# Four tokens to a partition for q and k, and seven block products for eight in the token mix, in a chunked attention and wave-MLP kernel

## The chip, the core and the metric

The kernel runs on one core of a Trainium2 chip. A core has TensorE (matrix products, PE in the profile, with its weight loads as PEld), VectorE (DVE), ScalarE (ACT), GpSimd (POOL) and SyncE (SP), a working memory of 128 partitions, and accumulator memory (PSUM) of eight banks, each of 512 f32 values per partition. Transfers run on 16 DMA engines; here GpSimd issues the loads that change f32 to f16, SP and ScalarE issue the rest. The metric is the time of one execution on the device in microseconds, lower is better; kernels are compared by medians of several executions.

## The reference

q, k and v have the shape 8 x 8 x 576 x 64 (batch, head, token, depth). Attention is done within chunks of 64 tokens; the result is laid out as batch x 576 x 512 and goes through a token and channel mixing block.

```python
scores = scale * np.matmul(q_c, k_c.transpose(0, 1, 2, 4, 3))   # chunks of 64 tokens
attn = np.exp(scores - max); attn = attn / (sum + 1e-9)
x = np.matmul(attn, v_c)                                        # then (8, 576, 512)
theta = x @ w_theta
zr, zi = x * np.cos(theta), x * np.sin(theta)
y = einsum('ts,bsd->btd', w_tok_r, zr) + einsum('ts,bsd->btd', w_tok_i, zi)
u = x + y
out = u + np.maximum(u @ w_ch, 0.0)
```

## The kernel before

The eight batches are worked in four pairs, 0 to 3. The 2 x 576 tokens of a pair are five groups: A and B are the first and the second 256 tokens of the pair's first batch, C and D those of its second batch, each two tiles of 128 tokens; M is the middle tile, the last 64 tokens of both batches.

Nothing is scheduled by a planner at run time. The text `ORDER` (line 16) lists every step, and the loop at line 769 issues them in that order; each engine runs its own instructions in the order of the list and waits for the others by semaphores. A step reads `name.pair+group.banks`, so `L.0C.1.2` is the step L for group C of pair 0 with PSUM banks 1 and 2. A digit after the name is a part: for most steps half of the heads (0 or 1) or one of the two tiles.

A group goes through these steps, in the names of the list:

- `q`, `k` (load_qk, line 172) and `v` (load_v, line 204): loads on GpSimd's queue, eight of them in flight at a time. q and k come with two adjacent tokens on a partition, 128 partitions, so that a packet holds two tokens of a head (256 B as f16); v comes one token to a partition in three loads per group. From the second pair on each load first copies a recent reciprocal (`gate`, line 166), which holds the queue back until that attention is done. q and k of a group share a buffer from a pool of ten, which also serves raw weights, outputs of the last pairs and, where they are used, differences of z.
- `L` or `T` or `N` (qk_t, line 284): transposes of q and k on TensorE. L is the long form, 32 transposes of a 128x64 piece; T is the small form, 64 transposes of 64x64, four of which fit side by side on the array; N is for M. `tq`, `tkA`, `tkV` (qk_copy, line 327) bring the results out of PSUM on VectorE or ScalarE.
- `S` (scores, line 345), `e` (exps, on ScalarE), `V` (attn: products with v and a column of ones), `n` (norm, on VectorE: a reciprocal and a multiplication, giving x).
- `X`, `Q` (turn: x transposed, in the long and the small form), `xA`, `xV` (its copy), `H` (x times w_theta), `g` (cosine and sine on ScalarE), `z` (two products on VectorE).
- `Y` (line 542; `YA` to `YM` by source group): the token mix. A group's output takes 18 matmuls of 128x128 by 512 columns (two tiles, each four tiles of tokens for the real and four for the imaginary part, and one for M); `Y.pM` takes 18 on half the array. `y` (add_x, line 680) adds x from PSUM, giving u, on VectorE.
- `U`, `R` (turn u, long and small), `uA`, `uV`, `W` (u times w_ch), `w` (relu_add, line 685), `s`, `sA` (stores issued by SP and by ScalarE).

`lw`, `TW`, `twV`, `twA` load, transpose and copy the token weights; `lt`, `ct` and `lc` handle w_theta and w_ch; `pe` and `pg` load ScalarE's tables for exponentials and for sines ahead of time; `D.n` issues n matmuls of zeros, which compute nothing. The steps `jw`, `j`, `K` and `r` (lines 592 to 674) exist in the code but are not in the list before. Functions touched by the change are shown here.

## Time and profile before

| | us |
|---|---|
| median of three runs | 206.74 (206.2 to 206.82) |
| the profiled execution | 205.98 |
| its span, first to last instruction | 204.2 |
| TensorE, VectorE, ScalarE, GpSimd busy | 192.3, 126.0, 115.6, 89.3 |
| granted TensorE clock, mean | 0.995 |

The span is cut into 40 slices of 5.1 us on the page; a digit there is the busy share of an engine in tenths. In lists of groups, "128x1024 f16<-128x1024 f32 x14 | 17.0, 1224" means 14 instructions that write 128 partitions of 1024 f16 values from f32 values, busy for 17.0 us in all, 1224 ns each; what follows is the engine's idle time before them and what ended it. "issue" stands for time in which an engine waited for nothing that the profile shows. Busy time of TensorE is modelled from pipelined instructions; the distance from one step's first matmul to the next one's is the better price of a step. The packed trace also records each DMA packet and the landing of each load.

### The profile page before, as it was taken

How to read it: one execution, taken by the hardware profiler on the slowest of the kernel's cores; microseconds unless marked ns; L12 is line 12 of the kernel's file. 1: busy time of each engine (PE TensorE's matmuls, PEld its weight loads, DVE VectorE, ACT ScalarE, POOL GpSimd, SP SyncE). 2: the span in 40 equal slices, each digit the busy share in tenths (PEclk: the TensorE clock that was granted, in tenths of full speed). 3: DMA queues.
4: the chain of work that ended last, by engine and by line, in shares of the span. 5: the costliest groups of instructions: out<-in, count | busy, mean ns of one | idle time of the engine just before them, and what ended most of it. 6: DMA issues, size and time to landing. Idle time of an engine off the chain costs nothing.

```text
span 204.2 us, 7908 instructions
## 1 busy us (share of the span) xinstructions
PE 192.3 (94%) x3584; PEld 102.8 (50%) x3584; DVE 126.0 (62%) x226; ACT 115.6 (57%) x142; POOL 89.3 (44%) x130
## 2 busy tenths in 40 slices
PE   7977999999997799999999999999999999999991
PEld 2344556656464365544654645445555544454440
DVE  0335696667364587924467886589666768643662
ACT  2044996678985378960759836498960857030120
POOL 7889495649989289999403502230400000000000
PEclk9999999999999999999999999999999999999997
DMA  6999999999999989999904993940723002042546
GB/s 210 144 150 150 179 190 169 146 181 118 169 170 157 114 158 176 167 173 159 122 11 127 214 256 135 157 27 3 51 59 106 3 3 104 0 167 108 190 177 185
DMA packets 87009, 27.00 MB, mean 132 GB/s; under 512 B 80064, under 2 KB 81984, under 8 KB 86976
## 3 DMA queue, kind: packets, MB, share of 16 engines
q0 software_dynamic: 81264, 16.01, 93.2%
q1 hardware_dynamic: 3920, 7.08, 10.2%
q10 hardware_dynamic: 1792, 3.41, 4.6%
q8 instruction: 28, 0.46, 0.9%
q14 instruction: 5, 0.04, 0.0%
HBM read 33.06 MB, written 9.44 MB: 208 GB/s over the span
## 4 chain that ended last, share of the span: by engine, by line
PE 76%; DMA 13%; POOL 5%; issue 4%; DVE 0%; DVEq 0%; POOLq 0%
PE ps L564 29%; PE ps L478 27%; DMA v<-in_v_dram 7%; DMA qk<-in_k_dram 4%; PE ps L550 4%; PE ps L438 3%; PE ps L318 3%; PE ps L400 3%; PE ps L447 3%; POOL qk L197 3%; PE ps L366 2%; DMA out_dram<-o 1%; POOL v L221 1%; POOL wnat L232 1%; PE ps L301 1%
## 5 line engine op out<-in xcount | busy, mean ns | idle before, releaser
L564 PE MATMUL ps<-z,wT 128*128 128x512 f16 x288 | 65.6, 380 | 1.5 <-issue 1.5
L564 PEld LDWEIGHTS <-wT 128*128 128x128 f16 x288 | 26.9, 98 | 32.6 <-issue 1.8
L221 POOL DMA_DIRECT2D v<-in_v_dram x48 | 36.2, 766 | 7.0 <-DMA qk<-in_k_dram 3.3
L683 DVE TENSOR_TENSOR x<-ps,x 128x1024 f16<-128x1024 f32 (+1 forms) x22 | 22.5, 1028 | 25.2 <-PE ps L564 22.4
L478 PE MATMUL ps<-wtheta,xT 128*128 128x512 f16 x144 | 34.4, 380 | 0.1
L478 PE MATMUL ps<-wch,uT 128*128 128x512 f16 (+1 forms) x148 | 34.1, 374 | 0.0
L382 ACT ACTIVATE eT<-ps 128x1024 f16<-128x1024 f32 (+1 forms) x18 | 16.6, 928 | 25.8 <-PE ps L366 24.4
L693 DVE SCALAR_TENSOR_TENSOR o<-ps,x 128x1024 f32<-128x1024 f32 (+2 forms) x23 | 22.5, 990 | 10.7 <-PE ps L478 6.6
L461 ACT COPY uT<-ps 128x1024 f16<-128x1024 f16 (+1 forms) x16 | 14.4, 909 | 25.5 <-PE ps L447 12.5
L414 DVE TENSOR_TENSOR x<-ps,recip 128x512 f16<-128x512 f32 (+1 forms) x40 | 25.5, 638 | 1.4
L338 ACT COPY kT<-ps 128x1024 f16<-128x1024 f16 (+1 forms) x18 | 16.4, 927 | 15.9 <-PE ps L305 10.8
L492 ACT ACTIVATE cos<-ps,pihalf 128x1024 f16<-128x1024 f32 (+1 forms) x22 | 21.2, 965 | 6.1 <-PE ps L478 3.5
L169 POOL COPY seen<-recip 1x1 f32<-1x1 f32 x13 | 2.7, 210 | 45.9 <-DVE recip L412 45.9
L478 PEld LDWEIGHTS <-uT 128*128 128x128 f16 x148 | 13.7, 98 | 15.0 <-issue 0.4
L478 PEld LDWEIGHTS <-xT 128*128 128x128 f16 x144 | 12.9, 98 | 13.8 <-issue 0.2
L496 ACT ACTIVATE sin<-ps 128x1024 f16<-128x1024 f32 (+1 forms) x22 | 19.2, 873 | 0.0
L334 DVE COPY qT<-ps 128x1024 f16<-128x1024 f16 (+2 forms) x23 | 12.9, 569 | 6.4 <-PE ps L305 4.4
L197 POOL DMA_DIRECT2D qk<-in_q_dram x16 | 14.5, 905 | 2.3 <-issue 1.5
L412 DVE RECIPROCAL recip<-ps 128x8 f32<-128x8 f32 (+1 forms) x40 | 7.9, 197 | 12.2 <-PE ps L400 10.3
L197 POOL DMA_DIRECT2D qk<-in_k_dram x16 | 14.4, 900 | 1.0 <-issue 0.6
L137 ACT ACT_TABLE_LOAD x11 | 14.1, 1283 | 0.2
L461 ACT COPY xT<-ps 128x1024 f16<-128x1024 f16 (+1 forms) x13 | 11.8, 922 | 1.3 <-PE ps L447 1.0
(52 smaller groups left out, 204.5 us busy)
## 6 DMA issues: line engine op xcount, KB each, us to landing
qk<-in_q_dram POOLq DMA_DIRECT2D x16, 256.0 KB, 6.4
qk<-in_k_dram POOLq DMA_DIRECT2D x16, 256.0 KB, 6.5
out_dram<-o SPq DMA_DIRECT2D x8, 512.0 KB, 3.6
out_dram<-o ACTq DMA_DIRECT2D x6, 512.0 KB, 3.3
v<-in_v_dram POOLq DMA_DIRECT2D x40, 64.0 KB, 5.5
v<-in_v_dram POOLq DMA_DIRECT2D x16, 128.0 KB, 6.2
wraw<-in_moe_w_theta_dram SPq DMA_DIRECT2D x2, 512.0 KB, 3.8
out_dram<-o SPq DMA_DIRECT2D x8, 128.0 KB, 2.3
```

Of the source, the lines that this page charges most:

```text
L197: nc.gpsimd.dma_start(t.rearrange("p (h x) -> p h x", h=H)[:, hs], ap[2 * p + bb, :, s0 : s0 + GT, :].rearrange("h (p s) d -> p h (s d)", ...
L221: nc.gpsimd.dma_start(v16[rows, slot + tile, :, 0:D], v[2 * p + bb, :, t0 : t0 + m, :].rearrange("h s d -> s h d"),)
L338: nc.scalar.copy(out=t.rearrange("p x s c -> p x (s c)").rearrange("p x (c s) -> p x c s", s=2), in_=ps.rearrange("p x s c -> p x c s"),)
L382: nc.scalar.activation(out=eT.rearrange("p h r e c -> p (h r e) c"), in_=ps, func=AF.Exp, scale=scale)
L414: nc.vector.tensor_tensor(out=tokens(p, g, "x")[:, :, f * NE * D : (f + 1) * NE * D].rearrange("p c (h d) -> p c h d", h=NE), in0=psv[:, 0 ...
L461: (nc.vector.tensor_copy if how == "V" else nc.scalar.copy)(out=to.rearrange("p b (r c) -> p b r c", c=CH), in_=psv)
L478: nc.tensor.matmul(ps[:, a * DM : a * DM + cols.stop - cols.start], xT[:, b0 + a, db, :], weight[:, db, cols], start=(db == 0), stop=(db = ...
L492: nc.scalar.activation(out=cos[:, 0:n].rearrange("p a e -> p (a e)"), in_=pin, func=AF.Sin, bias=pihalf, scale=1.0,)
L496: nc.scalar.activation(out=sin[:, 0:n].rearrange("p a e -> p (a e)"), in_=pin, func=AF.Sin)
L564: nc.tensor.matmul(ps[:, a * DM : a * DM + DM], wT[:, kt, t0 : t0 + P], zs[bb], start=(done + k == 0), stop=(done + k == NK - 1),)
L683: nc.vector.tensor_tensor(out=u, in0=ps, in1=u, op=ALU.add)
L693: nc.vector.scalar_tensor_tensor(out=o, in0=ps[:, 0 : n * m].rearrange("p (j d) -> p j d", j=n), scalar=0.0, in1=u, op0=ALU.max, op1=ALU.add,)
```

## The change

There are three parts.

**Loads of q and k.** For groups A to D the new steps `qF` and `kF` put four adjacent tokens on a partition. q takes partitions 0 to 63 of the buffer and k partitions 64 to 127. A load has 512 packets of 512 B instead of 1024 packets of 256 B, with the same bytes. M is loaded as before.

**Transposes.** Step `F` is a small form for this layout, 64 transposes of 64x64; `FL` is a long form, 32 transposes of a 128x64 piece that holds q above k. Scores read q with a stride of four tokens, and the copies and exponentials restore the order. `tqA` copies q on ScalarE.

**Token mix.** In pair 0 it stays as it is, by source group. In pairs 1 to 3 the two batches are mixed together, as a 2x2 matrix of 256-token blocks of the weights times the 2x2 blocks of z (A, C above B, D), by seven block products, as Strassen's method does, in Winograd's form. `jw` forms four sums of weight blocks once; `ja` to `jd` form four differences of z per pair on VectorE; `Ka` to `Kg` are the products of eight matmuls each, b, c and d of which add M's column in two more, and `Km` adds it for the fourth block; products add up in the same PSUM banks, and the takes `ra` to `rh` add them to x on VectorE in between. M itself is mixed by `Y` as before. These functions are unchanged and now used (cut to their core):

```python
ZSUMS = {"a": ("C", "A"), "b": ("D", "a"), "c": ("D", "C"), "d": ("B", "b")}   # first - second
PRODUCTS = {  # PSUM block, weight block or sum, z block or difference, M's column for (block row, batch)
    "a": ("x", (0, 0), "A", None),  "b": ("y", (0, 1), "B", (0, 0)),
    "c": ("z", 3, "D", (0, 1)),     "d": ("w", (1, 1), "d", (1, 0)),
    "e": ("z", 0, "a", None),       "f": ("x", 1, "b", None),
    "g": ("x", 2, "c", None),       "m": ("x", None, None, (1, 1)),
}
TAKES = {  # group whose x is added to, PSUM block
    "a": ("A", "x"), "b": ("A", "y"), "c": ("C", "x"), "d": ("C", "z"),
    "e": ("D", "z"), "f": ("D", "x"), "g": ("B", "x"), "h": ("B", "w"),
}
def weight_sums(i):   # jw.00, jw.01; put is one VectorE tensor_tensor into wsum[k], 128x1024
    if i == 0: put(0, w_block(1, 0), w_block(1, 1), ALU.add); put(2, w_block(0, 0), w_block(1, 0), ALU.subtract)
    else:      put(1, wsum[0], w_block(0, 0), ALU.subtract);  put(3, w_block(0, 1), wsum[1], ALU.subtract)
def step(p, g, bank):  # product k
    ...
    for a in range(2):
        ...
        for i, (wt, zt) in enumerate(terms):   # 4 terms of a product, and one of M's column
            nc.tensor.matmul(ps[:, a * DM : a * DM + DM], wt, zt,
                             start=fresh and i == 0, stop=i == len(terms) - 1, ...)
def step(p, g):        # take k
    nc.vector.tensor_tensor(out=u, in0=st[p]["ps_k", frm], in1=u, op=ALU.add)
```

**The order.** The whole list is another one. It loads and transposes B, C and D of the first pair ahead of M and A, has 36 dummy matmuls for 42, and ends with whole groups where the list before ended with halves. The diff, with the list cut:

```diff
--- before.py
+++ after.py
@@ -14,45 +14,47 @@
 ORDER = """
-q.0B k.0B init.00 D.12.0 lt.00 ctV1.00 ctV0.00 q.0M k.0M id.00 D.19.0 L0.0B.0.1 tkA0.0B
-L1.0B.7.6 tq1.0B N0.0M.5 tkV0.0M tkA1.0B q.0A N1.0M.1 tq0.0B S1.0B.6 tkV1.0M tq0.0M D.3.2
-S0.0M.2 e1.0B tq1.0M S0.0B.4 v.0B D.4.0 V1.0B.0 e0.0B e0.0M V0.0B.2 n0.0B k.0A S1.0M.6 D.4.5
-L1.0A.5.4 v.0M n1.0B L0.0A.3.2 tq1.0A e1.0M Q0.0B.0 tq0.0A tkA1.0A S1.0A.6 Q1.0B.4 tkA0.0A
...
-W1.3C.0 y.3M R.3M.4 uV1.3D s.3B R0.3D.2 w.3A y0.3C R0.3C.6 sA.3A W1.3D.1 w1.3C uV.3M w1.3D
-W.3M.0 uA0.3C s1.3C uA0.3D W0.3D.7 s1.3D w.3M s.3M w0.3D W3.3C.1 s0.3D w3.3C s3.3C W2.3C.0 w2.3C
-s2.3C
+init.00 D.12.0 qF.0B kF.0B id.00 D.14.0 F1.0B.0.1 qF.0C kF.0C F0.0B.2.3 tq1.0B tkA1.0B S1.0B.0
+FL.0C.4 tq.0C qF.0D kF.0D D.5.6 FL.0D.6 v.0B e1.0B tq0.0B tkA.0C S.0C.4 e.0C lt.00 tq.0D ctV0.00
+ctV1.00 v.0C D.5.4 V1.0C.4 tkA0.0B q.0M k.0M V0.0C.0 tkA.0D S.0D.2 n0.0C e.0D S0.0B.6 v.0D n1.0C
+N0.0M.0 tq0.0M qF.0A X.0C.1 N1.0M.2 e0.0B xV.0C V0.0B.6 tkA0.0M tqA1.0M V1.0B.4 n1.0B H.0C.0
+kF.0A n0.0B lw.00 v.0M V1.0D.4 v.0A FL1.0A.6 n1.0D lw.02 tkA1.0M pg.00 g.0C FL0.0A.2 V0.0D.4
+tq1.0A qF.1C tq0.0A tkA0.0A kF.1C n0.0D X0.0B.0 tkA1.0A S1.0M.2 X.0D.1 xV0.0B xV.0D TW.00.4
+twV.00 q.1M e1.0M TW.01.6 twV.01 S1.0A.0 z.0C qF.1A S0.0A.2 e0.0A V1.0M.4 n1.0M e1.0A H0.0B.5
+S0.0M.6 V0.0A.2 e0.0M n0.0A H.0D.0 V1.0A.6 V0.0M.4 pg.00 g.0D n1.0A kF.1A g0.0B YC.0C.2 n0.0M
+X.0M.4 xV.0M X0.0A.0 xV0.0A qF.1B TW.02.6 kF.1B H.0M.1 twV.02 Q1.0B.4 xA1.0B FL.1C.6 H1.0B.0
...
+qF.3A kF.3A sA.1B q.3M V0.3C.6 V0.2B.4 Y.1M.1 z.2A uA.1A V1.3C.2 n0.2B n0.3C Q.2B.4 xA.2B y.1M
+n1.3C Ka.2A.6 Q.2M.0 Q.3C.2 ja.2C s.0M s.1C xV.3C F.3A.5.4 xA.2M H.2M.0 tqA.3A k.3M ra.2A g.2M
+Ke.2C.2 W.1A.0 z.2D jb.2D re.2D w.1A tkA.3A S.3A.4 pe.00 e.3A z.2M jc.2D Kf.2C.6 H.2B.4 H.3C.0
+pg.00 g.2B Kc.2D.2 rc.2C F.3D.4.5 g.3C tkA.3D V1.3A.0 Kg.2D.6 U.1M.5 z.2B rd.2C v.3M n1.3A rg.2B
+tqA.3D V0.3A.0 n0.3A R.1D.2 uA.1D Y.2M.4 uV.1M V1.3B.0 n1.3B T.3M.2 tqA.3M y.2M X.3A.5 xA.3A
+Km.2D.6 tkV.3M W.1D.0 s.1A v.3D S.3D.2 V0.3B.4 rf.2D H.3A.6 pe.00 e.3D n0.3B w.1D R.2C.4 Q.3B.2
...
+pg.00 g.2B Kc.2D.2 rc.2C F.3D.4.5 g.3C tkA.3D V1.3A.0 Kg.2D.6 U.1M.5 z.2B rd.2C v.3M n1.3A rg.2B
+tqA.3D V0.3A.0 n0.3A R.1D.2 uA.1D Y.2M.4 uV.1M V1.3B.0 n1.3B T.3M.2 tqA.3M y.2M X.3A.5 xA.3A
+Km.2D.6 tkV.3M W.1D.0 s.1A v.3D S.3D.2 V0.3B.4 rf.2D H.3A.6 pe.00 e.3D n0.3B w.1D R.2C.4 Q.3B.2
+jd.2B xV.3B z.3C Kb.2B.0 rb.2A uA.2C g.3A W.1M.2 w.1M H.3B.4 g.3B V1.3D.0 n1.3D V0.3D.6 Kd.2B.2
+n0.3D Q.3D.0 z.3A S.3M.4 pe.00 e.3M W.2C.6 rh.2B V0.3M.2 n0.3M ja.3C V1.3M.5 xA.3D R.2B.3 uA.2B
+H.3D.0 pg.00 g.3D W.2B.2 n1.3M w.2C X.3M.4 xA.3M Ka.3A.6 w.2B z.3D jb.3D R.2D.0 R.2A.2 uA.2A
+uA.2D z.3B sA.2C s.2B Ke.3C.4 ra.3A re.3D H.3M.3 g.3M z.3M W.2A.0 W.2D.2 w.2D jd.3B w.2A Kf.3C.6
+rc.3C s.1D s.2D Kc.3D.4 Kd.3B.2 Kb.3B.0 jc.3D Kg.3D.6 rh.3B rb.3A R.3A.0 rd.3C uA.3A rg.3B
+Y.3M.2 sA.1M R.3B.0 uA.3B R.3C.4 Km.3D.6 y.3M rf.3D W.3A.2 W.3B.0 w.3A uA.3C sA.2A w.3B R.3D.6
+uA.3D s.3A R.2M.2 uA.2M W.3C.4 W.3D.6 w.3C w.3D R.3M.0 sA.3B W.2M.2 w.2M s.3C s.3D uA.3M W.3M.0
+w.3M sA.2M s.3M
 """.split()
@@ -174,6 +176,16 @@
         gate(p)
         if (p, g) not in nats:
             nats[p, g] = nat.tile([P, 2, 2 * DM], FP16, name="qk16", tag="nat")
+        if plain is None:
+
+            t = nats[p, g][half[which]].rearrange("p a x -> p (a x)")
+            nc.gpsimd.dma_start(
+                t.rearrange("p (h x) -> p h x", h=H),
+                (q, k)[which][2 * p + bb, :, s0 : s0 + GT, :].rearrange(
+                    "h (p s) d -> p h (s d)", s=4
+                ),
+            )
+            return
         t = nats[p, g][:, which]
         hs = slice(0, H) if f is None else slice(f * NE, f * NE + NE)
         ap = (q, k)[which][:, hs]
@@ -285,7 +297,38 @@
         n = 1 if g == "M" else 2
         ne, e0 = part(f)
         t = nats[p, g]
-        if form != "small":
+        if form == "four":
+
+            t = t.rearrange("p a x -> p (a x)")
+            pss = [psum(b, 1, FP16)[:, 0 : ne * 4 * CH] for b in banks]
+            pss = [ps.rearrange("p (e s c) -> p e s c", e=ne, s=4) for ps in pss]
+            for e in range(ne):
+                for s in range(4):
+                    for w in range(2):
+                        for h in range(2):
+                            x0 = ((2 * (e0 + e) + h) * 4 + s) * D
+                            nc.tensor.transpose(
+                                pss[w][half[h], e, s],
+                                t[half[w], x0 : x0 + D],
+                                id16[half[w], half[w]],
+                            )
+        elif form == "four long":
+
+            form = "four"
+            t = t.rearrange("p a x -> p (a x)")
+            ps = psum(banks[0], 2, FP16)[:, 0 : ne * 4 * P]
+            ps = ps.rearrange("p (e s w c) -> p e s w c", e=ne, s=4, w=2)
+            for e in range(ne):
+                for s in range(4):
+                    for h in range(2):
+                        x0 = ((2 * (e0 + e) + h) * 4 + s) * D
+                        nc.tensor.transpose(
+                            ps[half[h], e, s].rearrange("p w c -> p (w c)"),
+                            t[:, x0 : x0 + D],
+                            id16,
+                        )
+            pss = [ps[:, :, :, w] for w in range(2)]
+        elif form != "small":
 
             if n == 2:
                 pss = [psum(b, 1, FP16)[:, 0 : ne * n * P] for b in banks]
@@ -328,16 +371,16 @@
         ps = st[p]["ps_qkT", g, f][which]
         _, nx, n, c = ps.shape
         name = "qk"[which] + "T"
-        t = tmp.tile([P, nx, n, c], FP16, name=name, tag=f"{name}{n}")
+        t = tmp.tile([P, nx, n, c], FP16, name=name, tag=f"{name}{min(n, 2)}")
         st[p][name, g, f] = t
         if how == "V":
             nc.vector.tensor_copy(out=t, in_=ps)
-        elif n == 1 or st[p]["form", g, f] == "plain":
+        elif which == 0 or n == 1 or st[p]["form", g, f] == "plain":
             nc.scalar.copy(out=t, in_=ps)
         else:
             nc.scalar.copy(
                 out=t.rearrange("p x s c -> p x (s c)").rearrange(
-                    "p x (c s) -> p x c s", s=2
+                    "p x (c s) -> p x c s", s=n
                 ),
                 in_=ps.rearrange("p x s c -> p x c s"),
             )
@@ -357,8 +400,13 @@
                         x, r0 = (r * ne + e, 0) if form == "small" else (e, r)
                         k0 = (n * r0 + cc) * CH
                         i0 = r0 * CH + cc * CH // 2
-                        kc = kf[half[h], x, k0 : k0 + CH]
-                        if n == 1 or form == "plain":
+                        if form != "four":
+                            kc = kf[half[h], x, k0 : k0 + CH]
+                        if form == "four":
+                            k0 = (2 * r + cc) * CH
+                            kc = kf[half[h], e, k0 : k0 + CH]
+                            qc = qT[half[h], e, :, k0 // 4 : k0 // 4 + CH // 4]
+                        elif n == 1 or form == "plain":
                             qc = qf[half[h], x, k0 : k0 + CH]
                         else:
                             qc = qT[half[h], x, :, i0 : i0 + CH // n]
@@ -378,7 +426,8 @@
             )
             return
         if st[p]["form", g, f] != "plain":
-            ps = ps.rearrange("p x (s i) -> p x i s", s=2)
+            s = 4 if st[p]["form", g, f] == "four" else 2
+            ps = ps.rearrange("p x (s i) -> p x i s", s=s)
         nc.scalar.activation(
             out=eT.rearrange("p h r e c -> p (h r e) c"), in_=ps, func=AF.Exp, scale=scale
         )
@@ -736,10 +785,15 @@
         "kP": lambda p, g, f: load_qk(p, g, 1, True, f),
         "ctA": lambda p, g, f: cast_theta(f, nc.scalar.copy),
         "ctV": lambda p, g, f: cast_theta(f, nc.vector.tensor_copy),
+        "qF": lambda p, g, f: load_qk(p, g, 0, None, f),
+        "kF": lambda p, g, f: load_qk(p, g, 1, None, f),
+        "F": lambda p, g, f, *banks: qk_t(p, g, f, "four", *banks),
+        "FL": lambda p, g, f, *banks: qk_t(p, g, f, "four long", *banks),
         "T": lambda p, g, f, *banks: qk_t(p, g, f, "small", *banks),
         "L": lambda p, g, f, *banks: qk_t(p, g, f, "long", *banks),
         "N": lambda p, g, f, *banks: qk_t(p, g, f, "plain", *banks),
         "tq": lambda p, g, f: qk_copy(p, g, f, 0, "V"),
+        "tqA": lambda p, g, f: qk_copy(p, g, f, 0, "A"),
         "tkV": lambda p, g, f: qk_copy(p, g, f, 1, "V"),
         "tkA": lambda p, g, f: qk_copy(p, g, f, 1, "A"),
         "S": scores,
```

## Prediction

> **What bounds the kernel now.** I read the 40 slices first, then the idle groups, the timeline's loads, the chain, and last busy time by stretch.
>
> ```profile
> PE   7977999999997799999999999999999999999991
> DVE  0335696667364587924467886589666768643662
> ACT  2044996678985378960759836498960857030120
> DMA  6999999999999989999904993940723002042546
> ...
> q0 software_dynamic: 81264, 16.01, 93.2%
> q8 instruction: 28, 0.46, 0.9%
> ...
> L564 PE MATMUL ps<-z,wT 128*128 128x512 f16 x288 | 65.6, 380 | 1.5 <-issue 1.5
> ```
>
> TensorE is full from the fifth slice on, apart from a dip at slices 13 and 14; VectorE and ScalarE have room everywhere. Before that, DMA is full and TensorE partly runs dummies. So three things make the time: how late the loads let TensorE start, how much it has to do, and where it is held.
>
> ```profile
> 31.13 0.69 POOL L221 DMA_DIRECT2D v<-in_v_dram  x1 [0.24 <-DMA qk<-in_q_dram]
> 32.67 0.68 POOL L221 DMA_DIRECT2D v<-in_v_dram  x1 [0.85 <-DMA qk<-in_k_dram]
> 34.12 0.89 POOL L221 DMA_DIRECT2D v<-in_v_dram  x1 [0.77 <-DMA qk<-in_q_dram]
> 35.62 0.68 POOL L221 DMA_DIRECT2D v<-in_v_dram  x1 [0.62 <-DMA qk<-in_k_dram]
> ```
>
> GpSimd waits here for the load eight places back, so these starts show one q or k load landing every 1.50 us.
>
> ```profile
> 61.77 1.29 issue
> ...
> 66.65 1.52 issue
> ```
>
> This is the dip. In the chain TensorE waits for nothing the profile shows, each time shortly after a packet of the instruction queue (60.65 and 65.86 in the packet records; 28 packets of 16 KB for 7168 TensorE instructions, so 256 instructions each).
>
> ```profile
> 100.00:130.00 30.00, 30.00 (x661) 15.86 (x659) 21.25 (x37) 20.12 (x24) 6.79 (x11) 1.00 0.84 141
> 130.00:160.00 30.00, 30.00 (x671) 15.71 (x673) 20.58 (x35) 19.46 (x21) 3.97 (x7) 1.00 0.38 62
> ```
>
> Columns three to five are TensorE, its weight loads and VectorE: VectorE has 9 us free in 30.
>
> **How I add up.** I price every TensorE step by its spacing in the timeline: 0.216 us per 512-column matmul (8 in 1.73), 1.06 for a "long" transpose of a q/k group, 0.55 for a "small" one, 0.27 for 32 scores, 0.19 for half an attention, 0.45 and 0.27 for turns of two tiles, 2.06 for the middle rows. Without dummies the order before comes to 172.9 us and ends at 199.5, so 26.6 us are lag: start minus the work done before it. The lag is 17.4 at 28 us, 19.0 at 61, 22.4 at 71 (the two holds, 1.6 and 1.7), and then grows by 4.3 to the end. The sum is made against the span of 204.2 us; the profiled execution took 205.98, the median of the runs is 206.74.
>
> **Token mix.** Three pairs go from 72 + 18 matmuls to 64 + 18 (seven products of eight, plus eight for the middle column): 24 fewer, 24 x 0.216 = **-5.2**. What VectorE gets for it: per pair 4 differences of 128x2048 f16 and 8 takes of 128x1024 from PSUM in place of 4 additions. A take is the 1.22 us addition. A difference is bounded by two rows of 1024 f16 (2 x 0.68 = 1.37) and by the same without the second fixed part (about 1.2); I take 1.22. With the four weight sums (at 0.68; at most 1.22 if their strides run like f32 rows): 3 x (4 x 1.22 + 4 x 1.22) + 2.7 = 32 us. Nine q copies move to ScalarE (-6 on VectorE, +9 there). Its cover is the 9 us in 30: VectorE comes from 126 to some 153 us busy. From the second pair's product c to the end its durations sum to 91 us against TensorE's 94, but rows in sequence overlap by some 0.07 us (59.27 to 59.88: 0.61 apart for 0.68), 8 us over the 110 operations left: 85 to 90% used, not the bound. But the products reuse banks: f waits for take a, g for c, m for g, and c for take e. Walking the last 31 us of TensorE's order with these prices I find no wait; at the second pair's product a 0.6 us. I charge **+0.8** (0 to +5): behind a TensorE instruction that waits, all its later work is queued.
>
> **Four tokens.** A load keeps its bytes (512 KB read, 256 KB written) and has 512 packets for 1024. Is it packets or bytes that take 1.50? The token weights, 288 KB in packets of 1152 B, land 1.43 apart, which is 413 GB/s read against 350; q and k at that rate take 1.27. The other end: packet records show 32, 42 and 107 ns for 128, 256 and 1152 B, so about 60 for 512; with two in flight per engine as now, 32 packets take 1.03. Above: half the partitions are written, and if that costs what the fewer packets save, 1.50. The half-partition loads of v (512 packets of 128 B, 0.42 apart) show no such loss against 0.87 for a full one. I take 1.30, being nearest to the weights' row. The Trainium skill (DMA: Bandwidth & Descriptors, Specifications) asks for 512 B or more for line rate and gives about 27 GiB/s per engine; by it a load would take an estimated 1.13 us, 1.4 us less in the sum below. The row of 1.50 for 256 B packets is already at three quarters of that rate. GpSimd issues a half-partition load in 0.70 for 0.90; it waits for landings anyway.
>
> **Order at the start.** Before the token weights (landed at 23.7) the new order puts q, k of C and D and v of C and D: 4 x 1.30 + 2 x 1.75 more, v of M and A (3.6) fewer, 4 x 0.2 quicker: 23.7 + 5.2 + 3.5 - 3.6 - 0.8 = 28.0, some 0.3 more since eight loads in flight are too few for small ones. There TW.00 has 9.1 us of work before it: lag 19.2. The next to be held is attention of A, whose v lands three v-steps later, at 31.2, with 11.5 us before it: **lag 19.7** against 17.4, so **+2.3** (+0.1 with loads of 1.03, +3.9 with 1.50). Dummies (42 to 36) lie inside this wait. Later loads keep their gates on GpSimd (a copy of a reciprocal); the tightest, q and k of A in the fourth pair, are let go 8.9 us of TensorE work before their transpose, against 5.0 to 7.7 us from issue to landing. The z differences share the pool of ten buffers with them; each buffer they take was done with at least 7 us of work earlier.
>
> **Transposes.** Before: 5 long, 11 small; after: 9 long, 7 small: 4 x (1.06 - 0.55) = +2.0, middle groups +0.2. Turns: three more groups by the long form and fewer split, +0.6. In all +2.8, and with the mix **-2.4**: 170.5 us.
>
> **Changes of tile size.** Between 64-wide and 128-wide steps the trace loses about 0.09 us (V 0.15 and then 0.24; H 1.73 and 1.82), net 0.05 over all. The order has 92 such changes for 82: **+0.5**.
>
> **Holds at instruction blocks.** The holds come where 256 instructions pass in 1 to 4 us while DMA is full. The new order has 6724 TensorE instructions; in the loaded stage the shortest block holds 4.8 us of work, most 6 to 8. I leave 0.8 of 3.2: **-2.4** (0 to -3.2). The Trainium skill (Runtime: NRT & Kernel Launch, Instruction fetch mechanics) also has blocks of 16 KiB, but calls their cost mostly hidden; by that these holds are something else and may stay.
>
> **ScalarE.** Table loads of 1.28 us go from 11 to 15 (four exponentials or sines now follow the other kind); +5 us on an engine with 80 free. The nearest, ahead of the C scores of the second pair, has 5.7 us of matmuls beside it. I cost it at nothing; uncovered it would be 1.28 each.
>
> **End.** The last addition is 128x512 (0.69) where it was 128x256 (0.42), behind two stores of 512 KB: **+0.3**. SP issues them one behind another, some 0.5 us each.
>
> **Sum:** -2.4 + 0.8 + 2.3 + 0.5 - 2.4 + 0.3 = **-0.9**: span 203.3, 205.1 for a profiled execution (1.8 lie around the span), and from the median 206.74, which lies 0.8 above that execution, **205.8**.
>
> **Rivals.**
> - *Loads near 1.03 us.* For it: the packet records. Against: 1152 B packets gain little. It gives 8 x 0.27 = 2.2 less: 203.6. (By the 1.13 of the Trainium skill's page on DMA it would be an estimated 204.4; no run shows it.)
> - *VectorE paces the products (slower).* Place: the twelve PSUM reuses. Each take queues behind a 1.22 us operation; if it is late by that at four to five of twelve, 5 x 1.22 less what is charged, some +4.1: 209.9. It decides from 2.3 us of waits on (0.8 + 0.9 + 0.6). For it: VectorE goes from 70% to nearly 90%. Against: the walk.
> - *The holds stay as they were:* +2.4, 208.2. For it: DMA is still full there. Against: fewer dense blocks. (If fetches are hidden, as the Trainium skill's page on the runtime says, the holds have another cause, and this is the case.)
> - *Four tokens do nothing* (1.50 per load): 8 x 0.2 = 1.6 later, partly under other waits, some 1.0: 206.8, no change.
>
> **How the numbers follow.** Forecast 0.37 (own range 204.6 to 206.8), loads 0.22, VectorE 0.22, holds 0.10, nothing 0.09. A measurement here tells 0.3% (0.6 us). Faster: 0.30 of the forecast and the loads' 0.22, 0.52. Same: 0.05 of the forecast and 0.09, 0.14. Slower: the rest, 0.34. The range leaves out a tenth on each side: from loads near 1.03 with no VectorE wait (202.4) to VectorE's case (209.9).
>
> **What would show it.** Right: q/k loads 1.25 to 1.35 apart; TW.00 at 28 to 29 us; waits of matmuls on VectorE under 2 us together; no "issue" of a microsecond between 40 and 80 us; VectorE near 160 us busy. Wrong: TW.00 before 26, or TensorE waiting on takes in the last 80 us.

## The result, and the profile after

| | before | after |
|---|---|---|
| median of 20 executions each | 206.34 (202.96 to 207.67) | 207.38 (206.12 to 209.15) |
| the profiled execution | 205.98 | 206.32 |
| its span | 204.2 | 204.1 |
| TensorE, VectorE, ScalarE, GpSimd busy | 192.3, 126.0, 115.6, 89.3 | 191.7, 153.6, 124.7, 82.5 |
| granted TensorE clock, mean | 0.995 | 0.985 |

The ratio is 1.0118 (95% interval 1.0083 to 1.0154): the changed kernel is some 1.2% slower, where 0.4% faster was predicted. The predicted 205.8 is 1.6 us too low; the range held the time, the direction was wrong. Medians, here and below, are over all executions, while ratios leave out those more than 1.5% above the fastest of their kernel.

The page of the changed kernel, in 40 slices and by group:

```profile
PE   7967769999999999999999999999999999999990
DVE  0024858777848898988898798997788889988661
PEclk9988999999999999999999999999999999999997
DMA  6999999999999999999672839920080008111566
...
q0 software_dynamic: 64880, 16.01, 83.1%
...
L702 PE MATMUL ps<-z,wT 128*128 128x512 f16 x72 | 18.9, 380 | 0.0
L702 PE MATMUL ps<-zsum,wsum 128*128 128x512 f16 x72 | 16.9, 380 | 0.0
L613 PE MATMUL ps<-z,wT 128*128 128x512 f16 x72 | 16.7, 380 | 0.0
```

The dip at slices 13 and 14 is gone, and no product of the token mix (L702) had an idle microsecond ahead of it. Packets fell from 81264 to 64880. New is the beginning: TensorE at 6, 7, 7 and 6 in slices 3 to 6, which were 7, 7, 9 and 9 before, and a clock of 8 tenths in slices 3 and 4, which was 9.

GpSimd's timeline of the changed kernel:

```profile
11.38 0.68 POOL L233 DMA_DIRECT2D v<-in_v_dram  x1 [0.45 <-DMA qk<-in_q_dram]
12.68 0.68 POOL L233 DMA_DIRECT2D v<-in_v_dram  x1 [0.62 <-DMA qk<-in_k_dram]
14.02 0.68 POOL L195 DMA_DIRECT2D qk<-in_q_dram  x1 [0.66 <-DMA qk<-in_q_dram]
...
17.06 1.35 POOL L195 DMA_DIRECT2D qk<-in_k_dram  x2 [0.88 <-DMA v<-in_v_dram]
18.40 2.45 POOL L233 DMA_DIRECT2D v<-in_v_dram  x3
20.84 0.70 POOL L182 DMA_DIRECT2D qk<-in_q_dram  x1
```

The first starts show, as in the prediction, one q or k load landing every 1.30 to 1.34 us (by the landings in the trace: 9.77, 11.09, 12.40, 13.74 us). For each large load that lands, GpSimd issues a small one (v of C, then M), so that the eight loads in flight hold less and less. From 17.7 us on GpSimd no longer waits for a landing. It issues loads of 64 and 128 KB (as f16) one behind another, at 0.67 to 1.0 us each, and they land as fast: when q of A, the next large one, is issued at 20.84, three loads are in flight, by their landings. So two things follow each other: eight small loads in flight hold little, and then GpSimd's issuing is the limit. What DMA moved in the meantime is in the last column of the busy time by stretch. Before:

```profile
15.00:25.00 10.00, 8.69 (x220) 5.30 (x219) 5.86 (x16) 6.96 (x14) 6.80 (x10) 1.00 1.65 163
25.00:35.00 10.00, 10.00 (x146) 5.91 (x146) 7.58 (x17) 8.21 (x13) 8.10 (x11) 1.00 1.71 182
```

After:

```profile
15.00:25.00 10.00, 7.64 (x205) 5.16 (x204) 6.20 (x13) 6.39 (x10) 8.61 (x13) 0.89 1.61 116
25.00:35.00 10.00, 8.04 (x182) 5.22 (x180) 7.74 (x17) 7.78 (x12) 7.37 (x13) 1.00 1.55 189
```

The third column is TensorE's busy time, the last three are the granted clock, the DMA share (over 1, since packets overlap on an engine) and GB/s: 116 GB/s for 163 between 15 and 25 us, though the slices show DMA busy throughout. The same view from 18 to 20 us has 77 GB/s. TensorE, full from 25 us on before, is at 8.04 of 10 until 35. What it waits for stands in its timeline:

```profile
27.30 1.08 PE L325 MATMUL ps<-id,qk 128*64 128x128 f16 x32 [1.33 <-DMA qk<-in_k_dram]
...
29.58 0.26 PE L414 MATMUL ps<-qT,kT 64*64 64x64 f16 x8 [0.62 <-ACT kT L381]
...
30.27 1.52 PE L278 MATMUL ps<-id,wnat 128*128 128x128 f16 x20
```

k of A landed at 27.16, the two halves of the token weights at 28.64 and 30.35; TW.00 (the last line) started at 30.3, where 28 to 29 was predicted. But there is no idle time ahead of it. TensorE waits for k of A (lag 18.8 at 25.6 us, 20.2 at 27.3) and then for ScalarE's copy of it, so that TW.00 starts with a lag of 21.2; behind TW.00 and TW.01 it is 21.6. The token weights, by which the prediction reckoned the start, hold TensorE for 0.4 us at most.

The lag, counted as in the prediction (start of a step less TensorE's work before it at its unit prices, without dummies), in us, at the first step from a time on; the columns from e2 on are experiments below (e17 and e18 have zeros put in at 38 and 37 us; in e18 the first step from 36 us on stands behind them):

| at | before | after | e2 | e5 | e12 | e17 | e18 |
|---|---|---|---|---|---|---|---|
| 28 us | 17.7 | 20.4 | 16.1 | 16.1 | 15.7 | 20.7 | 17.4 |
| 36 | 18.0 | 22.4 | 16.9 | 16.7 | 17.2 | 22.5 | 21.6 |
| 45 | 18.7 | 23.0 | 17.3 | 17.4 | 19.3 | 25.7 | 21.9 |
| 60 | 19.2 | 23.4 | 17.8 | 17.5 | 20.3 | 26.8 | 22.3 |
| 80 | 23.1 | 24.2 | 23.4 | 18.2 | 23.7 | 27.8 | 25.7 |
| 100 | 23.5 | 24.8 | 23.8 | 21.1 | 26.0 | 28.4 | 26.1 |
| 140 | 25.3 | 26.7 | 25.6 | 23.2 | 28.0 | 31.7 | 28.2 |
| 190 | 26.6 | 28.1 | 27.0 | 24.6 | 30.2 | 33.0 | 29.7 |
| work | 172.9 | 170.5 | 172.9 | 174.5 | 170.9 | 170.5 | 172.9 |

So the changed kernel has 2.4 us less to do, starts 4.4 us later, and gets 3 us of that back between 60 and 80 us, where the kernel before is held.

### The profile page after: what moved, and what is told of

Read it like the earlier page. It is cut to its first block, busy times and chain, and to the rows that moved or that the text cites. A ratio compares the mean times of both kernels' runs of the same rounds, so it can differ in the third digit from the quotient of the medians.

```text
span 204.1 us, 7502 instructions
## 1 busy us (share of the span) xinstructions
PE 191.7 (94%) x3362; PEld 103.5 (51%) x3362; DVE 153.6 (75%) x241; ACT 124.7 (61%) x151; POOL 82.5 (40%) x134
## 4 chain that ended last, share of the span: by engine, by line
PE 83%; DMA 8%; POOL 4%; issue 1%; DVE 1%; ACT 0%; DVEq 0%; POOLq 0%
PE ps L527 30%; PE ps L702 21%; PE ps L613 8%; DMA v<-in_v_dram 5%; PE ps L487 4%; PE ps L599 4%; PE ps L325 3%; PE ps L449 3%; PE ps L496 3%; DMA qk<-in_k_dram 3%; PE ps L414 3%; POOL qk L182 2%; PE ps L310 2%; PE ps L278 2%; POOL v L233 1%
## 5 line engine op out<-in xcount | busy, mean ns | idle before, releaser
L527 PE MATMUL ps<-wch,uT 128*128 128x512 f16 x144 | 33.8, 379 | 0.0
L721 DVE TENSOR_TENSOR x<-ps,x 128x1024 f16<-128x1024 f32 x24 | 29.0, 1218 | 4.2 <-PE ps L702 3.8
L510 ACT COPY uT<-ps 128x1024 f16<-128x1024 f16 (+1 forms) x14 | 12.6, 922 | 26.4 <-PE ps L496 23.3
L742 DVE SCALAR_TENSOR_TENSOR o<-ps,x 128x1024 f32<-128x1024 f32 (+1 forms) x20 | 22.3, 1114 | 5.8 <-PE ps L527 5.1
L541 ACT ACTIVATE cos<-ps,pihalf 128x1024 f16<-128x1024 f32 (+1 forms) x22 | 21.1, 958 | 6.3 <-PE ps L527 4.2
L377 DVE COPY qT<-ps 128x1024 f16<-128x1024 f16 (+2 forms) x14 | 7.7, 563 | 17.6 <-PE ps L310 9.2
L702 PE MATMUL ps<-z,wT 128*128 128x512 f16 x72 | 18.9, 380 | 0.0
L702 PE MATMUL ps<-zsum,wsum 128*128 128x512 f16 x72 | 16.9, 380 | 0.0
L613 PE MATMUL ps<-z,wT 128*128 128x512 f16 x72 | 16.7, 380 | 0.0
L289 PE MATMUL ps<-zeros 128*128 128x512 f16 x36 | 12.0, 502 | 2.3 <-DVE pihalf L133 1.2
L702 PEld LDWEIGHTS <-wsum 128*128 128x128 f16 x96 | 8.9, 98 | 10.2
L702 PEld LDWEIGHTS <-wT 128*128 128x128 f16 x96 | 8.8, 98 | 9.5
```

The costliest lines, as they stand in the source:

```text
L510: (nc.vector.tensor_copy if how == "V" else nc.scalar.copy)(out=to.rearrange("p b (r c) -> p b r c", c=CH), in_=psv)
L527: nc.tensor.matmul(ps[:, a * DM : a * DM + cols.stop - cols.start], xT[:, b0 + a, db, :], weight[:, db, cols], start=(db == 0), stop=(db = ...
L541: nc.scalar.activation(out=cos[:, 0:n].rearrange("p a e -> p (a e)"), in_=pin, func=AF.Sin, bias=pihalf, scale=1.0,)
L613: nc.tensor.matmul(ps[:, a * DM : a * DM + DM], wT[:, kt, t0 : t0 + P], zs[bb], start=(done + k == 0), stop=(done + k == NK - 1),)
L702: nc.tensor.matmul(ps[:, a * DM : a * DM + DM], wt, zt, start=fresh and i == 0, stop=i == len(terms) - 1, skip_group_check=to in ("x", "z"),)
L721: nc.vector.tensor_tensor(out=u, in0=st[p]["ps_k", frm], in1=u, op=ALU.add)
```

## The experiments

Each was compared with the kernel before on the same chip; ratios are to it, with 95% intervals. The changed kernel stands at 1.0118 (1.0083 to 1.0154). us are medians. In the diffs of `ORDER` only what changes is shown.

### The three terms by themselves

**The 24 matmuls (e9).**

```
@@ product
+                if z is not None and not middle:
+                    terms.append((wt[:, 0, 0, a * P : a * P + P], zeros))
                 if middle:
```

> The changed kernel with the 24 matmuls put back that the seven products save: the four products without a middle term get one more matmul per tile, against a tile of zeros (it adds nothing), 8 per pair; differences, takes, loads and order stay. Theory: TensorE bounds the kernel from the second pair's products on, so 24 x 0.216 = 5.2 us come back in full: 207.4 + 5.2 = 212.6 (211.5 to 213.5). Rival: TensorE has slack there (it waits for differences, takes or banks anyway), and less than half comes back: 207.5 to 210.

213.55 us, ratio 1.0429 (1.0362 to 1.0496): 3.1% above the changed kernel, 6.4 us give or take 1.6. The theory holds: what the products save on TensorE comes back in full; the interval includes 5.2.

**The differences on VectorE (e10).**

```
@@ z_sum
-            t = nat.tile([P, 2, 2, DM], FP16, name="zsum", tag="nat")
-            st[p]["zsum", k] = t
-            nc.vector.tensor_tensor(out=t, in0=a, in1=b, op=ALU.subtract)
+            st[p]["zsum", k] = a
```

> The changed kernel without the four differences of z per pair (a product takes the tile that the difference would have begun with, so the output isn't the reference's): 12 VectorE operations of 128x2048, 14.6 us, are left out, and their buffers. Theory: VectorE isn't what holds the changed kernel (its trace has no wait of note of a matmul on VectorE): 206.4 to 207.4. Rival: VectorE paces the products: 2.5 us or more faster, below 205.

This kernel leaves the differences out and so computes something else. 207.78 us, ratio 1.0116 (1.0032 to 1.02), the changed kernel's own. Its page has VectorE 13.4 us lighter:

```profile
PE 191.3 (93%) x3362; PEld 104.0 (50%) x3362; DVE 140.2 (68%) x229; ACT 124.6 (60%) x151; POOL 82.7 (40%) x134
```

VectorE doesn't pace the kernel. The changed kernel's own list of TensorE's waits says the same; behind the first microseconds, those on VectorE are 1.2 us together, all ahead of 25 us:

```profile
PE ps L325 <- DMA qk<-in_k_dram: 2.6, 2, 1.3
...
PE ps L344 <- DVE x L463: 0.7, 1, 0.7
PE ps L487 <- DVE x L463: 0.3, 1, 0.3
PE ps L527 <- DVE xT L510: 0.2, 1, 0.2
```

(The numbers are us in total, times, and the longest.)

**Four tokens, taken back in the new order (e11).**

```
@@ ORDER
-... qF.0B kF.0B ... F1.0B.0.1 qF.0C kF.0C ... FL.0C.4 ... F.2A.2.6 ...
+... q.0B k.0B ... L1.0B.0.1 q.0C k.0C ... L.0C.4.5 ... L.2A.2.6 ...
```

> The changed kernel's order with q and k two tokens to a partition again (loads of 1024 packets; small transposes by the old small form, long ones by the old long form, and those of 2A, 3A and 3D long for small since their banks aren't neighbours: 3 x 0.5 = 1.5 us of TensorE more). Theory: the four tokens are worth the shorter loads: 8 q/k loads before the token weights x 0.17 = 1.4, and 0.2 of issue each, so the lag at 36 us is 23.7 to 25 for 22.3 and the time 207.4 + 1.5 + 1.4 to 2.4 = 210.3 to 211.3. Rival: the loads' length doesn't matter in this order, since eight in flight run dry either way: only the forms count, 208.5 to 209.3.

211.0 us, ratio 1.0278 (1.0193 to 1.0362), 3.3 us above the changed kernel (1.9 either way), of which 1.5 are the three long forms; the lag at 36 us is 23.3 for 22.4. The theory's time came, and what is left for the four tokens is some 1.8 us, where eight loads 0.17 shorter make 1.4. The lag at 36 us stayed below the theory's 23.7 to 25, so that the start shows 0.9 of it only; where the rest arises is open.

**Four tokens alone, in the order before (e2).**

```
@@ ORDER
-q.0B k.0B init.00 ... L0.0B.0.1 ... T.1D.0 ... T.1B.4 ... T.1C.2 ...
+qF.0B kF.0B init.00 ... FL0.0B.0 ... F.1D.0.1 ... F.1B.4.5 ... F.1C.2.3 ...
```

> The order before, with the four-token loads and their transposes alone (small form for small, long for long). Theory (a load is bound by its bytes): loads land 1.30 us apart for 1.50, the start gains 0.5 to 1.5 us, the time is 0.5 to 1.5 us under the kernel before. Rival (loads to half of the partitions, or their transposes, cost something): no change or up to 2 us slower. Rival (packets bind): loads near 1.0 us apart and 2 to 3 us faster.

206.7 us, ratio 1.0051 (1.0011 to 1.009): not faster, against the theory. The lag is 1.1 to 1.6 us smaller until 60 us, and then the chain shows what takes it:

```profile
59.76 0.53 PE ps L411 x49
60.28 1.27 issue
61.55 0.32 PE ps L411 x15
61.87 2.06 PE ps L596 x18
63.93 0.64 PE ps L307 x64
64.57 0.29 PE ps L446 x28
64.86 3.17 issue
```

The holds before were 1.29 and 1.52 in the chain, 3.3 us in lag; here they are 1.27 and 3.17, 4.9 in lag. TensorE, earlier at the same dense stretch, is held longer.

**The same with fewer instructions there (e5).**

```
@@ ORDER, against e2
-F.1B.4.5 F.1C.2.3 ... F.2A.6.7
+FL.1B.4 FL.1C.2 ... FL.2A.6
```

> The order of before with q and k four tokens to a partition (as in e2_four_tokens_only, 206.7), and three transposes of q and k between 55 and 65 us (1B, 1C and 2A) by the long form: 64 TensorE instructions each for 128, at 1.06 us for 0.55. Theory: the two holds of e2 (1.3 us at 60.3 and 3.2 us at 64.9, with no wait shown) come from instruction blocks passed too fast while DMA is full; with 192 fewer instructions in that stretch they go or shrink below 1 us in all, the lag at 80 us is 18.5 to 20.5 for 23.3, and the time is 206.7 - 4.4 + 1.6 = 203.9 (203 to 205). Rival: the holds have another cause (a wait that the profile doesn't show) and stay; then the three forms add 1.6: 207.5 to 208.5.

206.5 us, ratio 1.0063 (1.0019 to 1.0106). The theory is right on the holds and wrong on the time; the rival is wrong on both. The chain of e5 has no hold between 55 and 81 us and then one at the next small transpose:

```profile
60.60 0.64 PE ps L411 x63
61.24 2.06 PE ps L596 x18
63.31 0.89 PE ps L322 x32
...
81.39 0.52 PE ps L307 x63
81.91 1.58 issue
```

192 instructions fewer took both holds away and brought the lag at 80 us to 18.2. Where the holds lie shows the rest. Of TensorE's matmuls and weight loads in the trace, 2235 and 2491 start before the matmuls behind the two holds of the kernel before, 2231 and 2487 in e2, 2995 in e5. That is 179 to 187 above a multiple of 256 each time, and each hold ends 2.3 to 3.3 us behind the start of a 16 KB packet of the instruction queue. So a hold is a wait for the next block of 256 instructions; with fewer of them in the stretch there was none. The smaller lag didn't bring the time: there are 1.6 us of longer transposes, a new hold of 1.9 in lag, and 4.5 us by which the lag grew after 80 us otherwise (3.6 in e2).

### What a late start costs

**A known delay in the changed kernel (e17) and in the kernel before (e18).**

```
@@ ORDER, changed kernel, 38 us
-... YC.0C.2 n0.0M X.0M.4 ...
+... YC.0C.2 n0.0M D.12.0 X.0M.4 ...
@@ ORDER, kernel before, 37 us
-... tkA.0D tq.1A S.1A.6 ...
+... tkA.0D tq.1A D.12.3 S.1A.6 ...
```

> The changed kernel with 12 matmuls of zeros, which compute nothing, put ahead of one step at 38 us: TensorE is made 12 x 0.216 = 2.6 us later there, nothing else is touched. It asks what a microsecond of lag at the start is worth at the end. Theory: it carries through, since no engine and no load holds the changed kernel behind it: 207.4 + 2.6 = 210.0 (209.3 to 210.7), final lag 31. Rival: later waits take it up (loads and copies come as they came, and TensorE waits for them less): 207.4 to 208.7.

> The kernel before with the same 12 matmuls of zeros at 37 us, ahead of the scores of A in the second pair. Theory: part of the 2.6 us is taken up by the two holds at instruction blocks at 61.8 and 66.7 us, which TensorE then reaches later: the holds fall from 3.3 us to below 1, and the time rises by 0 to 1.2 only, 206.2 to 207.6. Then an early start is worth less in the order before than its lag says. Rival: the holds keep their length and it carries through: 208.4 to 209.4.

e17: 212.19 us, ratio 1.035 (1.0291 to 1.0409). e18: 209.96 us, ratio 1.024 (1.0184 to 1.0296). In e18 the zeros wait 1.1 us for a copy to leave their bank, so TensorE is 3.1 us late at 40 us, and its profiled span is 3.1 longer (207.3). In the changed kernel it is 2.6 late at 40, and the lag at the end is 4.9 larger: two waits, 0.9 at 55 us and 1.4 at 133, came on top. Both are holds at instruction blocks, with nothing shown that TensorE waits for (1719 and 4787 instructions before them, 183 and 179 above a multiple of 256), where the changed kernel has none. The holds of the kernel before shrank, but kept more than half:

```profile
65.04 0.81 issue
...
69.11 1.29 issue
```

In both kernels a microsecond of lag at 37 us costs at least one at the end. In the changed kernel the delay carries through, as the theory has it, but the time is above its 209.3 to 210.7, since the holds came on top; in the kernel before the rival holds. By the ratios both cost some 4.8 us (2.3 and 2.4%), in e18 1.8 more than its profile shows; that rest stays open. So nothing behind the start takes up the 4.4 us by which the changed kernel is later at 36 us. That an earlier start would win as much isn't shown by a delay.

**The clock at the start (e3).** In the changed kernel's profile TensorE runs at half speed for one stretch:

```profile
13.90:17.30 3.40, 3.40 (x37) 1.98 (x34) 0.78 (x2) 1.01 (x1) 1.59 (x3) 0.51 2.34 151
```

There the transposes of D took 1.84 us for 1.08. More zeros were put into the waits ahead of it:

```
@@ ORDER
-... S1.0B.0 FL.0C.4 ... V1.0D.4 v.0A ...
+... S1.0B.0 D.5.7 FL.0C.4 ... V1.0D.4 D.6.3 v.0A ...
```

> The changed kernel with 11 more dummy matmuls in two waits of the start (five after the first scores, six ahead of the transposes of A). Theory (in the changed kernel the TensorE clock falls to half for 3.4 us in the start of most executions): the mean granted clock rises from 0.985 to 0.99 or more in every execution, and the median falls by 0.5 to 1.2 us against the changed kernel's 207.4. Rival (the start is held by loads, the clock costs nothing): the clock rises, the median stays within 0.4 us.

208.07 us, ratio 1.0109 (1.0057 to 1.016). The rival's time came. The clock was restored (1.000, 9 in every slice), the lag at 36 us fell by 0.9 only, to 21.5, and was 0.4 above the changed kernel's at the end. The halved clock makes up 0.9 us of the late start at most, and the profile of e9 says less. It has the same steps up to there, and its clock is 1.00 from 8 to 36 us:

```profile
27.07 1.08 PE L325 MATMUL ps<-id,qk 128*64 128x128 f16 x32 [2.64 <-DMA qk<-in_k_dram]
```

TensorE comes to the transposes of A earlier and waits 2.64 us for k of A instead of 1.33; its lag at 36 us is 22.1 for 22.4. So the halved clock at 13.9 us costs 0.3 at most, and the landing of k of A sets the start: in e9 at 26.93 us, in e3 at 26.16.

**The loads in another order (e4).**

```
@@ ORDER, loads of the first pair behind those of B
-qF.0C kF.0C ... qF.0D kF.0D ... v.0B ... v.0C ... q.0M k.0M ... v.0D ... qF.0A ... kF.0A ... lw.00 v.0M ... v.0A
+qF.0C kF.0C qF.0D v.0B kF.0D v.0C qF.0A q.0M k.0M kF.0A v.0D lw.00 v.0M v.0A
```

> The changed kernel with the loads of the first pair in another order on GpSimd's queue: the four small loads of M and the v loads are put between the large ones of q and k, and A comes ahead of M's k. Theory (with eight loads in flight, a row of small ones lets the DMA engines run dry, which holds the token weights until 30.4 us): no gap of over 2 us between landings, token weights landed by 28.5, and the time 1.5 to 3 us under the changed kernel. Rival (TensorE's start is held by something else): landings earlier, time within 0.5 us.

208.68 us, ratio 1.014 (1.009 to 1.0189), by the ratios 0.5 us above the changed kernel: the theory's time didn't come. k of A landed 4.1 us earlier (23.07 for 27.16) and the second half of the token weights 1.6 earlier (28.71 for 30.35), but k of D, now behind v of B, 1.6 later (16.85 for 15.22). TensorE waited 3.3 us for it, and by the busy time by stretch its clock was then halved for two stretches:

```profile
13.90:17.20 3.30, 0.31 (x6) 0.31 (x8) 0.00 (x0) 0.31 (x1) 2.10 (x4) 0.96 1.95 175
17.20:20.60 3.40, 2.27 (x65) 2.07 (x60) 1.75 (x3) 1.17 (x2) 2.81 (x4) 0.50 1.75 134
20.60:24.00 3.40, 3.36 (x85) 1.68 (x85) 1.10 (x3) 1.38 (x3) 3.40 (x6) 0.54 1.81 158
```

At 23 us the lag was 19.9 for 18.4, at 36 us 23.7 for 22.4. The earlier loads of A and of the token weights were of no use by then: what TensorE needs first decides, not the mean rate.

### Looking for an order that has both

**Products undone by order (e1, e8).** e1 puts the groups' matmuls as before where the products b, c, d and g stood; e8 rearranges the steps behind the first 150 for them.

```
@@ ORDER
-... Ka.1A.4 ... Kg.1D.4 ... Kc.1D.0 ... rg.1B ... Kb.1B.6 ... Kd.1B.2 ...
+... Y.1D.4 ... Y.1C.0 ... Y.1A.6 ... Y.1B.2 ...
```

> The changed kernel with the token mix of pairs 1 to 3 put back to four group outputs of 18 matmuls; the start, the loads and the rest of the order stay. Theory (the mix gives what was reckoned, the loss lies at the start): 24 more matmuls at 0.216 us, so 5.2 us slower than the changed kernel, 211 to 213 us, VectorE busy down from 154 to about 130 us. Rival (VectorE's differences and takes eat the gain in the changed kernel): 206 to 208 us, no more than 1 us from the changed kernel.

> The changed kernel's first 150 steps and its four tokens, with the token mix of the last three pairs by groups of 18 matmuls as before (no differences, no takes), and the steps after the first 150 rearranged for it, since in e1_mix_by_groups (221.95) the groups stood where products had stood and TensorE waited 9.8 us. Theory: the seven products save their 24 matmuls of 0.216 and cost TensorE nothing: 207.4 + 5.2 = 212.6 (211.5 to 214), the lag at 36 us as in the changed kernel (22 to 23). Rival: the products cost in waits what they save, and the groups in a fitting order end at 207 to 209.5.

e1: 221.95 us, 1.0778 (1.0725 to 1.0832). e8: 227.32 us, 1.091 (1.0813 to 1.1008). Neither theory nor rival: work rose by 5.2 as it should, but nine waits of over 0.4 us behind 36 us cost some 10 us in e1 and some 8 in e8 (on sines and exponentials above all), and e8's span ends 8.8 us behind TensorE's last matmul (5.2 in the changed kernel). Another order is another kernel; e9 was made for this reason.

**Before's start with products (e6, e7, e12, e13).** e6 and e7 begin with before's first 50 steps, e12 and e13 with its first 90, in the four-token form; the rest is the changed kernel's work, rearranged.

```
@@ ORDER, e12: its start
-init.00 D.12.0 qF.0B kF.0B id.00 D.14.0 F1.0B.0.1 qF.0C kF.0C ...
+qF.0B kF.0B init.00 D.12.0 lt.00 ctV1.00 ctV0.00 q.0M k.0M id.00 D.19.0 FL0.0B.0 ...
```

> The same work as the changed kernel (seven products, four tokens), in another order: the first 50 steps are those of before's order (groups B, M, A of the first pair loaded and worked first, the token weights early, and before's dummies), the rest is rearranged behind it. Theory: the changed kernel lost its gain at the start; its TensorE starts are 22.3 us behind the work at 36 us, where e2 with before's start is 16.6 behind. With that start the lag at 36 us is 16.5 to 18.5, no hold of a microsecond comes between 40 and 80 us, and the time is 207.4 less 4 to 6: 201.5 to 203.5. Rival: the seven products can't be fed early (differences, banks, VectorE), and what the start gains is given back before 120 us: 206 to 208 with a final lag above 26.

> As e6_early_start, with another arrangement behind the same first 50 steps (work of the first and second pair mixed more closely, loads of the third pair in another order). Theory (the start decides): within 1.5 us of e6_early_start, 201.5 to 204. Rival (the fine arrangement decides): more than 2 us away from it.

> The same work as the changed kernel; the first 90 steps are those of before's order with four tokens (groups B, M, A of the first pair, the token weights, before's dummies: the part in which e2 and e5 are 16 to 17 us behind their work), the rest rearranged so that 64-wide and 128-wide steps change as seldom as possible (88 changes; e6 had 116, the changed kernel 93) and each store is issued right behind its addition (e6 and e7 left them to the end, 8 us after the last matmul). Theory: the start is what the changed kernel loses, and e6 and e7 failed by their changes of size, late stores and a start that was rearranged too: lag at 36 us 16.5 to 18, no hold of a microsecond, time 201 to 205. Rival: what the early start gains is given back behind it in waits on copies, loads or banks as in e6: final lag above 30 and 208 or more.

> As e12_before_start, with another arrangement behind the same first 90 steps. Theory: within 1.5 us of e12_before_start. Rival: more than 2.5 us from it, so that the fine arrangement decides and not the start.

214.39, 215.44, 212.56 and 215.12 us; ratios 1.0411 (1.0337 to 1.0485), 1.0513 (1.0452 to 1.0573), 1.0281 (1.0173 to 1.039), 1.0447 (1.0367 to 1.0527). All are slower than the changed kernel. e6 and e7 didn't have the early start: their lags at 36 us are 19.4 and 20.9. e7 lost 9.9 us in 105 changes between 64-wide and 128-wide steps behind 36 us (6.0 in 76 in the changed kernel) and nearly five more behind the last matmul, its stores being issued late. e12 did have the early start (17.2 at 36 us) and lost it to seven waits, together 6.2 us, on several causes:

```profile
PE ps L525 <- ACT eT L429: 1.7, 1, 1.7
PE ps L525 <- DMA wch<-in_moe_w_ch_dram: 1.3, 1, 1.3
PE ps L412 <- ACT kT L379: 1.2, 2, 0.6
```

Here the rival's time came about, with the lag at 190 us at 30.2. e13, with the same first 90 steps, lies 2.6 us from e12, as its rival had it: the same start doesn't make the same time.

**The start of e5 kept, products behind it (e14, e15, e16).** Seven products in the last pair, the last two, the last three. The first 167 steps are those of e5, and the next 57 too, but for two stores of the first pair (`sA.0A`, `s.0B`) that are put among them.

```
@@ ORDER, e14 against e5: two stores earlier, from 70 us on rearranged, and
-... H.1A.2 ... sA.0A ... Y.3A.6 ... Y.3B.2 ... Y1.3D.4 Y0.3D.4 ... Y1.3C.0 Y0.3C.1 ...
+... sA.0A H.1A.2 ... s.0B ... Ka.3A.6 ... Kb.3B.4 ja.3C ... Ke.3C.2 ... Kf.3C.6 ... Kc.3D.2 ... Kd.3B.4 ... Kg.3D.6 ... Km.3D.6 ...
```

> e5_four_tokens_long (before's order, four tokens, three long forms; 206.5, lag 18 at 75 us) with its first 70 us kept step by step, and the token mix of the last pair alone by seven products (8 matmuls fewer, 1.7 us), the steps after 70 us rearranged for it. Theory: TensorE bounds the kernel after 70 us, and the products can be fed from an early start: 206.5 - 1.7 = 204.8 (203.5 to 206). Rival: as in e12, what is rearranged loses more in waits on copies, loads and banks than the products save: 208 or more.

> As e14_one_pair, with seven products in the last two pairs (16 matmuls fewer, 3.5 us). Theory: 203 (201.5 to 205). Rival: 208 or more.

> As e14_one_pair, with seven products in the last three pairs, as in the changed kernel (24 matmuls fewer, 5.2 us). Theory: 201.5 to 203.5, and the lag at 75 us 18 to 19. Rival: 208 or more, with the lag growing by more than 8 us after 80 us.

210.77, 218.35 and 221.41 us; ratios 1.0222 (1.0184 to 1.0259), 1.0599 (1.0556 to 1.0642), 1.0728 (1.0674 to 1.0782). The rival's times came, worse with each pair, in part by waits that the rearranged steps have among themselves. The longest in e15 is for a load:

```profile
PE ps L308 <- DMA qk<-in_q_dram: 5.8, 1, 5.8
```

But these kernels lost e5's start as well. The two stores, of 512 KB each, go out at 49 and 55 us, where e5's first store goes out at 67, while the loads keep DMA busy. In e14 a load of k issued at 48.4 us landed at 57.5 (in e5 47.8 and 54.8), and TensorE waited for it:

```profile
57.62 1.98 PE L322 MATMUL ps<-id,qk 128*64 128x128 f16 x64 [1.55 <-DMA qk<-in_k_dram]
```

The lag at 75 us is 21 to 22 in all three, where e5 has some 18. So the question whether some order has before's start and seven products without waits isn't answered by these; none that was tried beats the kernel before.

## Why the prediction was wrong, step by step

The terms of the sum, against the two profiled executions (lag from the table):

| term | predicted | measured |
|---|---|---|
| work on TensorE (mix, transposes, turns) | -2.4 | -2.4 by the same prices; the mix's part confirmed by e9 |
| VectorE waits | +0.8 | 0 |
| start | +2.3 | +4.4 (22.4 for 18.0 at 36 us) |
| changes of tile size, after 36 us | +0.5 | +0.1 (76 at 0.079 for 68 at 0.087), other +0.5 |
| holds at instruction blocks | -2.4 | -3.3 |
| end, within the span | +0.3 | +0.6 (5.2 for 4.6 behind TensorE's last matmul) |
| around the span | 0 | +0.4 (2.2 for 1.8) |
| sum, profiled execution | -0.9 | +0.3; the executions differ by +0.34 |

- **Start: the step that failed.** It was to cost 2.3 us and cost 4.4; its size was wrong, and so was the load that it took to hold TensorE. The length of q and k loads (1.30) was right. The prediction added up loads as if DMA were always fed, with 0.3 us for "some 0.3 more since eight loads in flight are too few for small ones". The gap was some 2 us: 116 GB/s for 163 between 15 and 25 us, the token weights at 30.4 and not 28.0. And it reckoned the lag at the token weights (19.2) and at v of A (19.7), while k of A, just ahead of the weights on the queue, wasn't in the sum. By the sum's own lengths it would land at 25.1 (28.0 less two of 1.43), about when TensorE came to it (26.0). It landed at 27.16 and was what TensorE waited for: lag 20.2, and 21.2 behind the wait for its copy. Attention of A then stood at 21.8 and not at 19.7. e9, at the full clock, waits longer for the same load and ends up at nearly the same lag. That nothing behind the start takes such a delay up, which the sum took for granted, is what e17 and e18 show.
- **Holds:** right in cause and sign. The chain of the changed kernel has no "issue" of a microsecond between 40 and 80 us, and e5 and the places of the holds show that they are waits for blocks of instructions. Of the 3.2 us, 0.8 were to stay; none did. The Trainium skill (Runtime: NRT & Kernel Launch, Instruction fetch mechanics) calls the cost of instruction blocks mostly hidden; while DMA is full the runs don't agree (3.3 us before, 4.9 in e2), and with fewer instructions from 55 to 81 us they do (e5).
- **VectorE:** right in saying it doesn't bound; even the 0.8 was too much. It was busy for 153.6 us, as the sum had it (some 153; the list of signs says near 160). The rival that VectorE paces the products is refuted by e10. Its price of 4.1 us fits four late takes (4 x 1.22 - 0.8), not the five that are written, which make 5.3; and the lower end of the range, 202.4, is 0.4 below what its terms give (205.8 - 2.2 - 0.8). Nothing hangs on either.
- **Loads:** 1.30 to 1.34 refutes the rivals of 1.03 and of 1.50. By the Trainium skill (DMA: Bandwidth & Descriptors, Specifications) packets of 512 B would have given an estimated 1.13; the trace doesn't agree, 1.30 us for 512 KB is 403 GB/s read.
- **Mix:** -5.2 right (e9: 6.4 give or take 1.6).
- **End:** 0.3 too small by 0.7, with what lies around the span; why the part around it grew was not tried.
- **From the profiled execution to the others.** The changed kernel's median lies 1.06 above its profiled execution, that of the kernel before 0.36: 0.7 that the prediction had at 0. Over its 20 executions the mean granted clock runs from 0.974 to 0.999; the seven below 0.98 have a median of 208.45, the eight from 0.987 on 206.5. Ten of the 20 have a lower clock than the profiled one (0.985). The kept profiles of e1, e9, e10 and e17, which have the changed kernel's steps up to 36 us, show where: the halved clock stands in the start, at another place each time. It is at 27.7 us in e1, at 26.9 in e17, twice as long from 28.3 in e10, and nowhere in e9; the lags at 36 us are 22.8, 22.5, 24.2 and 22.1. So by these profiles the halved clock costs up to 2.1 us, by where it falls and for how long. e3, with 0.994 to 1.000 in its six, was no faster all the same, so that the 0.7 isn't shown to come from the clock alone.

The slower case that the prediction did list (VectorE, 209.9) wasn't the one that came. The case missing among the rivals was a start worse than the sum of its loads, 205.8 + 2.1 = 207.9; the forecast of -0.9 changes sign when the start is 0.9 us worse than added up.

## What to carry to other kernels

When loads are reordered, don't add their durations alone: check how many bytes the loads in flight hold at each place and how long their issue takes, since in a run of small loads the transfer rate fell from 163 to 116 GB/s while the busy row still showed 9. Price every load that stands ahead of the one reckoned with: here k of A held TensorE, and not the token weights behind it. In both kernels here a delay at the beginning was paid in full at the end, and a delay put in on purpose measures that in one run. Undoing a part by reordering an interleaved list measures the order, not the part; adding back its work in place (zeros, an idle product) measures the part.
